# A new order for the first batch's attention, with fillers in the free columns of a PSUM bank

## The chip, the core and the metric

The kernel runs on one NeuronCore of a Trainium2 chip. The metric is the device time of one execution in microseconds (us). The span that a profile shows is some 1.8 us shorter than this time. All times compared here are of runs in the fast state; the one slow run (730.63 us, at a granted clock of 0.735) is left out, and one single run of unknown state is marked as such.

One derived number is used throughout. In the traces of all runs but the slow one the granted clock of TensorE stands at 1.00 or at 0.50 and nowhere between, and each run lists its mean. So the time that a run spent at half clock is (1 - granted clock) x span x 2. A clock of 0.994 over 578 us is 6.9 us. The clock is listed to three places, which makes this good to about 0.6 us. Values up to 1.2 us need not be a stretch inside the program: in one trace the only half clock begins at the very end.

## The reference, cut to what matters

```python
B, H, S, D = 8, 12, 448, 64                 # d_model = 12 * 64 = 768
q_n, k_n = rmsnorm(q, g_q), rmsnorm(k, g_k) # over D
attn = softmax(q_n @ k_n^T / sqrt(D))
x    = (attn @ v), heads side by side       # (8, 448, 768)
u    = x + (x^T @ U @ V)^T                  # U: 448x32, V: 32x448
out  = u + relu(u @ w_ch1) @ w_ch2          # 768 -> 3072 -> 768
```

Inputs and output are float32.

## The kernel before

Attention of batch b+1 is woven between the matmuls of batch b's MLP, so that TensorE nearly always has work. Only the first batch's attention has no MLP beside it. That stretch, the first 45 us, is `head()`: a plan written by hand, a list of pieces in one order. Each engine takes its own instructions in that order. A tile number t stands for four heads: q, k and v of heads 4t to 4t+3. A pair number p is two heads. The pieces that matter:

```python
def load_w1(i):                 # a piece of the first MLP weight, issued by POOL
    c = (slice(0, 512), slice(512, 1024), slice(1024, 2048), slice(2048, 3072))[i]
    nc.gpsimd.dma_start(w1b[:, :, c], w1r[:, :, c])

def cast_v(t):                  # v of four heads, f32 -> bf16; POOL
    nc.gpsimd.tensor_copy(va_of(t)[:, :, :, 0:D], vts.pop(t).rearrange(...))

def weigh(p, hh):               # attention weights times v; PE; needs va and E
    ...
    if hh and p < 6:
        o = ps_mm.tile([P, 4, D + 1], FP32, tag="mm")
    ...
    else:
        o = ps_o.tile([P, 4, D + 1], FP32, tag="o")
    ...

def heat(n):                    # fillers: matmuls of zeros that keep PE busy
    if n:
        warm = ps_mm.tile([P, 512], FP32, tag="mm")
        for _ in range(n):
            nc.tensor.matmul(warm, cold[:, 0:P], cold[:, 0:512], start=True, stop=True)

def head():
    load(0, 2); load(1); load(2)        # q and k of tiles 0, 1, 2; queue of SyncE
    load_mix()                          # U and V
    load_v(0); load_v(1); load_v(2)     # v; behind all of the above
    load(3); load_v(3)
    setup()                             # memsets on POOL
    plan = [(heat, 16), ..., (reduce, 1, ALL, (1,)), (load_w1, 0), ...,
            (cast_v, 0), ..., (weigh, 0, 1), ...]
    for fn, *args in plan:
        fn(*args)
```

Other pieces: `squares`, `reduce` and `rsqrt` make the norms, `scale` applies them (VectorE), `turn` transposes on PE and `keep` copies the result to SBUF, `scores` and `expo` are the softmax's matmuls and exponentials. From the fifteenth pair on the transposes are done by DMA instead (`qkT<-qkn`), and the mixer's input `u` as well (`u<-ring`).

Of the kernel before, what the change touches and what calls it, by code (L numbers as in the profile page):

```python
# [9 lines left out]
FP32 = mybir.dt.float32  # L10
# [7 lines left out]
def kernel(  # L18
# [13 lines left out]
    nc = tc.nc  # L32
    B, H, S, D = q.shape
# [5 lines left out]
    P = 128  # L39
# [26 lines left out]
    ps_mm = ctx.enter_context(tc.tile_pool(name="ps_mm", bufs=3, space=bass.MemoryType.PSUM))  # L66
    ps_s = ctx.enter_context(tc.tile_pool(name="ps_s", bufs=2, space=bass.MemoryType.PSUM))
    ps_o = ctx.enter_context(tc.tile_pool(name="ps_o", bufs=1, space=bass.MemoryType.PSUM))

    ident = consts.tile([P, P], BF16, name="ident")  # L70
    w1b = consts.tile([P, KD, dh], BF16, name="w1b")
# [46 lines left out]
    cold = ring[:, 0, :]  # L118
# [104 lines left out]
    ALL = slice(0, HG)  # L223
# [83 lines left out]
    def weigh(p, hh):  # L307

        b = p // 6
        par, g = b % 2, b // 2 % 2  # L310
        E, va = E_of(p), va_of(p // 2)
        hl = 2 * (p % 2) + hh
        if hh and p < 6:
            o = ps_mm.tile([P, 4, D + 1], FP32, tag="mm")
        elif hh and p % 6 == 5:
            o = ps_s.tile([P, 4, D + 1], FP32, tag="s", name="o")
        else:
            o = ps_o.tile([P, 4, D + 1], FP32, tag="o")
        for i, off in enumerate(OFFS[par]):
            n = (i + 1) % 4 if par == 0 and g else i  # L320
            for kc in range(NJ):
                c = PAD + kc * S + off
                nc.tensor.matmul(o[:, n, :], E[:, hh, c:c + P], va[:, hl, kc, :],  # L323
                                 start=(kc == 0), stop=(kc == NJ - 1))
        outs[p, hh] = o
# [333 lines left out]
    def head():  # L659

        A, Bh = slice(0, 2), slice(2, 4)
# [11 lines left out]
        cast_u = lambda: nc.gpsimd.tensor_copy(Uc, Uf)  # L673
        pool = nc.gpsimd
        plan = [
            (heat, 16),
            (grow2,),
            (squares, 0, A, (0,), pool),
            (squares, 0, A, (1,)),
            (squares, 0, Bh, (0,), pool),  # L680
            (reduce, 0, A, (0,)),
            (reduce, 0, A, (1,)),
            (reduce, 0, Bh, (0,)),
            (rsqrt, 0, A),
            (squares, 0, Bh, (1,)),
            (scale, 0, 0, (1,)),
            (reduce, 0, Bh, (1,)),
            (scale, 0, 0, (0,)),
            (rsqrt, 0, Bh),
            (scale, 0, 1, (1,)),  # L690
            (turn, 0),
            (squares, 1, ALL, (0,)),
            (gain,),
            (keep, 0, 0, 1),
            (yield_port, 0, 1),
            (squares, 1, ALL, (1,)),
            (keep, 0, 1),
            (scale, 0, 1, (0,)),
            (heat, 4),
            (scores, 0, (0,)),  # L700
            (turn, 1),
            (squares, 2, ALL, (0,)),
            (reduce, 1, ALL, (0,)),
            (expo, 0, 0),
            (scores, 0, (1,)),
            (reduce, 1, ALL, (1,)),
            (load_w1, 0),
            (expo, 0, 1),
            (rsqrt, 1),
            (heat, 2),  # L710
            (scores, 0, (2,)),
            (scores, 0, (3,)),
            (keep, 1, 1),
            (keep, 1, 0),
            (scale, 1, 0, (1,)),
            (squares, 2, ALL, (1,)),
            (scale, 1, 0, (0,)),
            (expo, 0, 2),
            (scale, 1, 1, (1,)),
            (heat, 5),  # L720
            (scores, 1, (0,)),
            (turn, 2),
            (scale, 1, 1, (0,)),
            (expo, 0, 3),
            (cast_u,),
            (expo, 1, 0),
            (scores, 1, (1,)),
            (scores, 1, (2,)),
            (load, 4),
            (heat, 2),  # L730
            (turn, 3),
            (expo, 1, 1),
            (scores, 1, (3,)),
            (keep, 2, 0),
            (expo, 1, 2),
            (keep, 2, 1),
            (expo, 1, 3),
            (scores, 2, (0,)),
            (yield_port, 1, 0),
            (scores, 2, (1,)),  # L740
            (cast_v, 0),
            (expo, 2, 0),
            (expo, 2, 1),
            (reduce, 2, ALL, (0,)),
            (reduce, 2, ALL, (1,)),
            (setup_u, 0),
            (scores, 2, (2,)),
            (scores, 2, (3,)),
            (keep, 3, 1),
            (rsqrt, 2),  # L750
            (setup_u, 1),
            (setup_u, 2),
            (cast_v, 1),
            (load_v, 4),
            (expo, 2, 2),
            (keep, 3, 0),
            (weigh, 0, 1),
            (scale, 2, 0, (0,)),
            (yield_port, 1, 1),
            (weigh, 0, 0),  # L760
            (expo, 2, 3),
            (scores, 3, (0,)),
            (scale, 2, 0, (1,)),
            (normalise, 0, 0),
            (scores, 3, (1,)),
            (normalise, 0, 1),
            (expo, 3, 0),
            (turn, 4),
            (weigh, 1, 0),
            (setup_u, 3),  # L770
            (expo, 3, 1),
            (keep, 4, 0),
            (normalise, 1, 0),
            (keep, 4, 1),
            (load, 5),
            (scores, 3, (2,)),
            (weigh, 1, 1),
            (scores, 3, (3,)),
            (expo, 3, 2),
            (expo, 3, 3),  # L780
            (weigh, 2, 0),
            (normalise, 1, 1),
            (scores, 4, (0,)),
            (gather, 0),
            (expo, 4, 0),
            (gather, 1),
            (scale, 2, 1, (0,)),
            (weigh, 2, 1),
            (gathered, 1, 1),
            (gathered, 0, 1),  # L790
            (scores, 4, (1,)),
            (load_v, 5),
            (scores, 4, (2,)),
            (setup_v,),
            (spread, 1),
            (scale, 2, 1, (1,)),
            (turn, 5),
            (load_w1, 1),
            (normalise, 2, 0),
            (normalise, 2, 1),  # L800
            (expo, 4, 1),
            (weigh, 3, 0),
            (yield_port, 2, 1),
            (spreaded, 1),
            (gather, 2),
            (scores, 4, (3,)),
            (expo, 4, 2),
            (keep, 5, 0),
            (expo, 4, 3),
            (cast_v, 2),  # L810
            (keep, 5, 1),
            (normalise, 3, 0),
            (gathered, 2),
            (scores, 5, (0,)),
            (weigh, 3, 1),
            (load_w1, 2),
            (spread, 0),
            (squares, 3, ALL, (1,)),
            (weigh, 4, 1),
            (scores, 5, (1,)),  # L820
            (normalise, 3, 1),
            (expo, 5, 0),
            (spreaded, 0, 1),
            (scores, 5, (2,)),
            (weigh, 4, 0),
            (normalise, 4, 1),
            (expo, 5, 1),
            (gather, 3),
            (spread, 2),
            (squares, 3, ALL, (0,)),  # L830
            (normalise, 4, 0),
            (gathered, 3, 1),
            (scores, 5, (3,)),
            (spread, 3),
            (spreaded, 2),
            (reduce, 3),
            (gather, 4),
            (expo, 5, 2),
            (squares, 4, ALL, (0,)),
            (cast_v, 3),  # L840
            (first, 0, (0, 1, 2), True),
            (expo, 5, 3),
            (weigh, 5, 1),
            (spreaded, 3, 1),
            (weigh, 5, 0),
            (first, 1, (0, 1, 2, 3), True),
            (rsqrt, 3),
            (normalise, 5, 1),
            (normalise, 5, 0),
            (gather, 5),  # L850
            (scale, 3, 0),
            (gathered, 4, 1),
            (gathered, 5, 1),
            (spread, 4),
            (first, 0, (3,), False),
            (spreaded, 4, 1),
            (spread, 5),
            (first, 0, (4,), False),
            (spreaded, 5, 1),
            (first, 1, (4,), False),  # L860
            (first, 0, (5,), False),
            (first, 1, (5,), False),
            (scale, 3, 1),
            (load_w1, 3),
        ]
        for fn, *args in plan:
            fn(*args)
# [33 lines left out]

    def heat(n):
        if n:
            warm = ps_mm.tile([P, 512], FP32, tag="mm")
            for _ in range(n):
                nc.tensor.matmul(warm, cold[:, 0:P], cold[:, 0:512], start=True, stop=True)

    def volume(b):
        n = (384, 512)[b % 2]
# [46 lines left out]
```

## Time and profile before

| | before |
|---|---|
| time, three runs | 579.06 us (578.95 to 579.19) |
| span of the profile, granted clock | 576.9 us, 0.993 |
| first MLP matmul issued by the MLP itself (`ph`) | 45.07 us |
| v of heads 0 to 3 landed, cast | 20.08, 20.31 us |
| first `weigh` | 24.68 us |

The prediction below shows the page and the stretches of the head. Lines of instructions show start, length, line, operation, tiles; in brackets how long the engine idled before, and for what. POOL's instructions in order of time (start, length, line, operation, tiles; in brackets how long the engine idled before, and for what):

```profile
16.12 1.02 POOL L181 DMA_DIRECT2D w1b<-in_moe_w_ch_dram  x1
...
20.31 1.03 POOL L221 CAST va<-vt 112x1024 bf16<-112x1024 f32 x1
```

The first weight piece is issued at 16.12. And PE up to its first `weigh`:

```profile
24.36 0.39 PE L172 MATMUL pt<-ident,Tw 32*128 32x32 bf16 x8
24.68 1.55 PE L323 MATMUL o<-va,E 112*128 112x65 bf16 x25
```

### The profile page before, as it was taken

The numbers are of one execution on the slowest core, as the hardware profiler recorded it, in microseconds if no ns is written. First come the engines' busy times: TensorE is split into PE (matmuls) and PEld (weight loads), VectorE is DVE, ScalarE is ACT, GpSimd is POOL, SyncE is SP. The second block draws the span as 40 slices with busy tenths as digits, with TensorE's granted clock in tenths as the row PEclk, the third lists the DMA queues.
The fourth block names the chain that finished last, engine by engine and source line by source line (L and its number), as shares of the span: only waits on it lengthen the run. The fifth ranks groups of instructions, "written<-read, shape, count | busy, mean of one in ns | idle before, by whom it ended". The sixth has DMA issues, their size and how long they took to land.

```text
span 576.9 us, 11306 instructions
## 1 busy us (share of the span) xinstructions
PE 560.0 (97%) x4607; PEld 306.5 (53%) x4607; DVE 387.1 (67%) x755; ACT 281.4 (49%) x419; POOL 79.0 (14%) x124
## 2 busy tenths in 40 slices
PE   5799999999999999999999999999999999999997
PEld 2465556544565555544465555644456555654464
DVE  4885964799875787647776598747767487453442
ACT  4777543376621875166641676246661475302200
POOL 4772510100020000000020000000011000000010
PEclk9799999999999999999999999999999999999999
DMA  9999985544443555544525455555334441050021
GB/s 212 243 252 226 216 139 141 129 118 88 112 136 93 117 135 126 114 99 113 129 75 116 105 130 120 125 132 128 82 79 127 122 97 33 28 110 1 1 55 55
DMA packets 103648, 67.22 MB, mean 117 GB/s; under 512 B 54716, under 2 KB 102060, under 8 KB 103596
## 3 DMA queue, kind: packets, MB, share of 16 engines
q1 hardware_dynamic: 93988, 56.77, 42.0%
q0 software_dynamic: 9376, 9.44, 9.8%
q8 instruction: 36, 0.59, 0.4%
q10 hardware_dynamic: 232, 0.30, 0.2%
q14 instruction: 16, 0.13, 0.1%
HBM read 52.19 MB, written 11.01 MB: 110 GB/s over the span
## 4 chain that ended last, share of the span: by engine, by line
PE 87%; DVE 4%; DMA 4%; ACT 1%; issue 0%; POOL 0%; DVEq 0%; ACTq 0%
PE ph L538 36%; PE pb L463 10%; PE po L463 8%; PE o L323 8%; PE pe L463 7%; PE pa L463 7%; PE sc L297 7%; DMA w1b<-in_moe_w_ch_dram 3%; DVE qkn L253 2%; PE pu L376 2%; ACT E L302 1%; DVE ring L378 1%; DMA u<-ring 1%; PE pm L362 1%; PE pt L264 0%
## 5 line engine op out<-in xcount | busy, mean ns | idle before, releaser
L538 PE MATMUL ph<-u,w1b 128*128 128x512 bf16 (+1 forms) x1128 | 232.6, 354 | 2.7 <-DVE qkT L275 1.2
L302 ACT ACTIVATE E<-sc 112x896 bf16<-112x896 f32 x184 | 159.8, 914 | 61.1 <-PE sc L297 61.0
L538 PEld LDWEIGHTS <-w1b 128*128 128x128 bf16 x1128 | 102.9, 98 | 110.9 <-issue 23.1
L463 PEld LDWEIGHTS <-hT 128*128 128x128 bf16 x1080 | 101.1, 98 | 71.1 <-issue 9.0
L541 ACT ACTIVATE hT<-ph 128x384 bf16<-128x384 f32 (+1 forms) x95 | 51.5, 542 | 130.7 <-PE ph L538 128.6
L543 DVE TENSOR_SCALAR hT<-ph 128x512 bf16<-128x512 f32 (+1 forms) x93 | 57.9, 622 | 57.0 <-PE ph L538 56.7
L323 PEld LDWEIGHTS <-E 112*128 112x128 bf16 x1472 | 59.8, 99 | 14.7 <-DVE ring L340 1.1
L323 PE MATMUL o<-va,E 112*128 112x65 bf16 x1440 | 62.1, 196 | 0.0
L253 DVE TENSOR_TENSOR qkn<-qk,rstd 112x512 bf16<-112x512 f32 x84 | 56.1, 707 | 7.2 <-ACT rstd L245 3.8
L297 PE MATMUL sc<-qkT 64*128 64x448 bf16 x384 | 55.9, 360 | 3.8 <-ACT E L302 2.2
L570 POOL COPY scratch<-qkn 1x1 bf16<-1x1 bf16 x44 | 11.1, 252 | 316.1 <-DVE qkn L253 316.1
L463 PE MATMUL po<-w2b,hT 128*128 128x384 bf16 x288 | 52.8, 326 | 0.1
L239 DVE TENSOR_REDUCE rstd<-sq 112x16 f32<-112x1024 f32 x40 | 48.4, 1211 | 4.7 <-ACT sq L231 4.7
L463 PE MATMUL pa<-w2b,hT 128*128 128x384 bf16 x264 | 49.5, 326 | 0.0
L463 PE MATMUL pb<-Tw,hT 128*128 128x384 bf16 x264 | 48.0, 326 | 0.0
L231 ACT ACTIVATE sq<-qk 112x1024 f32<-112x1024 f32 x36 | 38.2, 1061 | 8.1 <-DVE rstd L239 5.2
L378 DVE TENSOR_TENSOR ring<-pu,ring 128x768 bf16<-128x768 f32 (+3 forms) x36 | 31.0, 864 | 14.4 <-PE pu L376 13.8
L333 DVE RECIPROCAL rec<-o 128x4 f32<-128x4 f32 x96 | 17.1, 179 | 33.5 <-PE o L323 33.1
L340 DVE TENSOR_TENSOR ring<-o,rec 128x256 bf16<-128x256 f32 (+1 forms) x96 | 37.6, 391 | 2.4
L498 POOL TENSOR_TENSOR o<-o,ring 128x384 f32<-128x384 f32 x11 | 12.6, 1144 | 161.3 <-DVE o L497 161.3
L297 PEld LDWEIGHTS <-qkT 64*128 64x128 bf16 x384 | 12.7, 94 | 35.6 <-issue 32.0
L478 ACT ACTIVATE pb<-pa 128x384 f32<-128x384 f32 x11 | 5.2, 475 | 49.6 <-PE pa L463 49.6
(104 smaller groups left out, 424.1 us busy)
## 6 DMA issues: line engine op xcount, KB each, us to landing
qk<-in_k_dram SPq DMA_DIRECT2D x21, 448.0 KB, 5.4
vt<-in_v_dram SPq DMA_DIRECT2D x20, 448.0 KB, 4.7
qk<-in_q_dram SPq DMA_DIRECT2D x19, 448.0 KB, 3.8
w2b<-in_moe_w_ch_dram POOLq DMA_DIRECT2D x6, 768.0 KB, 14.8
w1b<-in_moe_w_ch_dram POOLq DMA_DIRECT2D x2, 1536.0 KB, 17.6
out_dram<-o SPq DMA_DIRECT2D x15, 168.0 KB, 2.3
out_dram<-o SPq DMA_DIRECT2D x16, 144.0 KB, 2.1
out_dram<-o SPq DMA_DIRECT2D x15, 120.0 KB, 2.1
```

What stands on the lines that cost most here:

```text
L231: nc.scalar.activation(sqs[t, s][:, hs], qks[t, s][:, hs], AF.Square)
L239: nc.vector.tensor_reduce(rstds[t][:, s, hs].rearrange("p h j -> p (h j)"), sqs[t, s][:, hs].rearrange("p h (j d) -> p (h j) d", d=D), AX, ...
L253: nc.vector.tensor_tensor(qkn[:, s].rearrange("p j h d -> p h j d"), qks[t, s][:, hp].rearrange("p h (j d) -> p h j d", d=D), rstd[:, s, h ...
L297: nc.tensor.matmul(sc[:, hh, 0:S], kT[pp, kc * SP:kc * SP + P], qT[pp, :], start=True, stop=True)
L302: nc.scalar.activation(E_of(p)[:, :, PAD + kc * S:PAD + (kc + 1) * S], scs.pop((p, kc))[0:SP, :, 0:S], AF.Exp, scale=float(D) ** 0.5)
L323: nc.tensor.matmul(o[:, n, :], E[:, hh, c:c + P], va[:, hl, kc, :], start=(kc == 0), stop=(kc == NJ - 1))
L340: nc.vector.tensor_tensor(ring[:, r0:r0 + t1 - t0, d0:d0 + D], o[:, t0:t1, 0:D], rec[:, t0:t1].rearrange("p c -> p c ()").to_broadcast([P, ...
L378: nc.vector.tensor_add(xv, pu[rows, 0:n, 0:HALF], xv)
L463: nc.tensor.matmul(ps, lhs[:, c, :], rhs[:, c, :], start=first and c == 0, stop=last and c == NC - 1, skip_group_check=again)
L538: nc.tensor.matmul(ph, w1b[:, dc, hc * P:(hc + 1) * P], u[:, dc, :], start=(dc == 0), stop=(dc == KD - 1))
L541: nc.scalar.activation(hT[:, hc, 0:n], ph, AF.Relu)
L543: nc.vector.tensor_relu(hT[:, hc, 0:n], ph)
```

## The change

Its intent is a head that takes less time and does not hang on exact timings: the order of the pieces was searched with random delays on every engine and load. Fillers move from a rotating PSUM tile to free columns of the bank that holds the attention output, so that they take no tile from transposes; they are shorter (240 columns) and many more (87 for 29). The first weight piece is issued right behind POOL's memsets. The diff, cut to its core:

```diff
+    bank = ps_o.tile([P, 512], FP32, name="bank")
+    even = bank[:, 0:4 * (D + 1)].rearrange("p (i d) -> p i d", i=4)
+    warm = bank[:, 272:512]
...
-            o = ps_o.tile([P, 4, D + 1], FP32, tag="o")
+            o = even
...
-            (heat, 16),
+            (heat, 34),
+            (load_w1, 0),
             (grow2,),
-            (squares, 0, A, (0,), pool),
...
-            (squares, 0, Bh, (0,), pool),
+            (squares, 0, A, (0,)),
+            (squares, 0, Bh, (0,)),
...
             (reduce, 1, ALL, (1,)),
-            (load_w1, 0),
... (some 200 lines: the same pieces in another order; heat of 1 to 6 in 14 places;
     load_w1 1 and 2 before yield_port 2, 1)
     def heat(n):
         if n:
-            warm = ps_mm.tile([P, 512], FP32, tag="mm")
             for _ in range(n):
-                nc.tensor.matmul(warm, cold[:, 0:P], cold[:, 0:512], start=True, stop=True)
+                nc.tensor.matmul(warm, cold[:, 0:P], cold[:, 0:240], start=True, stop=True)
```

## The prediction

> **What bounds the kernel now.** I read the page first, then one-microsecond stretches of the first 45 us, then each engine's instructions in time order there, then the DMA queues. The change touches only the head of the program (batch 0's attention and mixing up to its MLP), so the first question is what the head is worth. Span, busy shares, the PE and clock rows of the 40 slices, and the chain that ended last:
>
> ```profile
> span 576.9 us, 11306 instructions
> PE 560.0 (97%) x4607; PEld 306.5 (53%) x4607; DVE 387.1 (67%) x755; ACT 281.4 (49%) x419; POOL 79.0 (14%) x124
> ...
> PE   5799999999999999999999999999999999999997
> ...
> PEclk9799999999999999999999999999999999999999
> ...
> PE 87%; DVE 4%; DMA 4%; ACT 1%; issue 0%; POOL 0%; DVEq 0%; ACTq 0%
> ```
>
> From slice 3 on (a slice is 14.4 us) PE is at nine tenths and the chain is PE. Nothing after the head changes in program order, so the end moves by as much as the MLP of batch 0 starts earlier or later, less what a DMA takes back. Only slices 1 and 2 have room, and slice 2 has a granted clock of 0.7. By stretches (columns: length, then busy us with instruction count of PE, PEld, DVE, ACT, POOL, then clock, DMA share, GB/s):
>
> ```profile
> 10.00:12.00 2.00, 1.84 (x14) 1.01 (x14) 0.84 (x2) 1.44 (x2) 0.18 (x1) 1.00 1.10 248
> ...
> 19.00:23.00 4.00, 2.09 (x20) 1.04 (x19) 4.00 (x6) 2.75 (x5) 3.39 (x6) 1.00 1.14 250
> ...
> 24.00:30.00 6.00, 6.00 (x81) 4.32 (x80) 3.90 (x12) 3.84 (x7) 1.28 (x4) 0.51 1.17 256
> ```
>
> From 12 to 24 us VectorE is full and PE only partly (2.09 of 4 us in 19 to 23). Then the clock falls to a half and from 24 to 30 PE is full while VectorE (3.90) and ScalarE (3.84) wait for it. So the head is bound by VectorE first, then by a PE at half clock, then by VectorE and PE together, until the MLP's matmuls begin at 45.07. The chain adds one DMA:
>
> ```profile
> 33.48 16.77 DMA w1b<-in_moe_w_ch_dram
> 50.24 0.05 issue
> ```
>
> This is the third piece of the first MLP weight, issued at 33.48, landed at 50.24. PE idles only 0.27 us for it, so it and the head's compute end almost together: shortening one alone gives little. Further on, the fourth piece (issued 40.85, 18.4 us to landing, so about 59.2) is first needed at 65.67, and the second MLP weight at 80.20. Those have 6 us and more of slack.
>
> **What the Trainium skill says.** (1) "TensorE: Matmul & The Clock Gate", Part 1: the clock is half or full, set from the array's activity in windows of about 3.4 us. The trace agrees: 0.50 from 24 to 29, after 4 us at 52% PE busy. (2) "PSUM — Partial Sum Buffer", "PSUM bank collisions raise a hardware error": two engines on the same bank and quadrant collide even at different columns; rule 2 says a starting matmul clears the accumulate bits of its whole bank. The fillers share a bank with the attention output, but in the new order the last filler comes before the first weigh(p, 0), so neither can occur; the trace of before has no such sharing. (3) "DMA: Bandwidth & Descriptors", "Issuing engines are not separate DMA queues": all issuers' transfers interleave on the same 16 engines. The trace agrees: from 24 to 28 us the software queue moved 0.49 MB and the hardware queue 0.48, where from 8 to 12 the hardware queue alone had 0.99.
>
> **The change part by part.**
>
> Fillers. Before: 29 matmuls of 512 columns, 8.53 us of PE. After: 34+4+5+6+1+2+2+4+4+5+4+1+6+6+3 = 87 of 240 columns. That is 20,880 columns against 14,848. Four warm fillers took 1.04 us and five 1.25, so 512 columns cost 0.21 us; 6,032 more cost 2.5 us of PE. They are spread up to the third pair's scores, where before had none after 19.4 us, and PE idles there for 1.9 of 4 us. They should remove most of the half-clock stretch. They also no longer take one of three rotating PSUM tiles that transposes and gathers need. On the path: I put 0.3 us for fillers that delay a real matmul.
>
> The half-clock stretch. PE's work from 24 to 29.6 takes 5.6 us at half clock, so some 2.8 at full. VectorE then becomes the limit. Its idle time is what can be won: 2.1 us from 24 to 30, and about 1.7 from 30 to 42.2, when the last pair is normalised (summed from one-microsecond stretches). Of these 3.8 us I take 3.0: at some hand-overs VectorE still waits.
>
> load_w1(0). It moves from 16.12 us to just behind the memsets on POOL, which end at 4.55. Before, the software queue's first packets came some 6 us after the issue, so now at about 10.5 us. From then on the two queues have half each. The tile that waits is q of heads 4 to 7, which ScalarE needs ahead of the first exponential:
>
> ```profile
> 12.36 1.06 ACT L231 ACTIVATE w2b<-Tw 112x1024 f32<-112x1024 f32 x1 [0.32 <-DMA Tw<-in_q_dram]
> ```
>
> It landed at 12.36, so at 10.5 it has 1.9 us to go at full rate, and 3.8 at half: it lands at about 14.3. Loads behind it come up to 3.2 us later (0.79 MB of the weight at 0.125 MB/us is 6.3 us of sharing). In the new order this square still stands before the first exponential in ScalarE's queue, so exponentials begin 1.9 us later. VectorE has one 1.2 us reduction to fill this with, so 0.7 to 1.9 us are lost; I take 1.3.
>
> load_w1(1), load_w1(2). POOL stood from 24.45 to 32.37 waiting for a scaling (yield_port(2, 1), 7.0 us of it listed as idle), and the third piece came after that. The new order puts the piece ahead of that wait: POOL has squares of tile 2 (2 x 1.9), casts (0.74 + 2 x 1.03) and the issues (2 x 0.9) after about 17.5 us, so the third piece goes out at 27 to 28, six us earlier, and lands near 44. Worth 0.27 us by itself, and the condition for any larger gain.
>
> Moves between engines. Two half squares go from POOL (1.03 us each) to ScalarE (0.63 each), at a time when ScalarE idles 1.7 and 1.2 us for VectorE. One copy of keys (0.38) goes from VectorE to ScalarE and two gathered copies (0.28 each) net the other way. Sum: nothing, to 0.2 us.
>
> Sum for the start of the MLP: -3.0 + 1.3 + 0.3 - 0.3 = -1.7 us, and the same at the end, since the slacks named above are larger. 579.06 - 1.7 = 577.4; I lean a little toward the search having found more density than I can see, and say 577.2.
>
> **The rivals.** (a) The early weight load costs more than it gives: the late tile starves ScalarE and VectorE from 12 to 16 us, PE idles long enough to lose its clock right there, and since the work behind is VectorE-bound nothing is regained: 579 to 581. For it: VectorE was full from 12 to 24, and the DMA share is above 1 throughout. Against: the loads behind have slack, ScalarE idled over 5 us later on. (b) The order is dense: no half clock, VectorE and ScalarE back to back, and the MLP starts 4 to 5 us earlier: 574 to 575. For it: 24 exponentials of 0.86 us are only 20.6 us of ScalarE; VectorE's work up to the last normalisation is some 31 us. Against: VectorE is short by 1.3 us already at 14 us. (c) The gain comes and the DMA takes it: the head is faster, but the fourth weight piece and the second weight stay at the transfer rate (all queues together moved what they could until 84 us). With 6 us of slack this bites only at the far end of (b).
>
> **Range and chances.** (a) gives the upper end, (b) the lower: 573.8 to 580.2. Two per cent is 11.6 us, a quarter of the whole head, which neither reaches. Faster 0.01, same 0.98, slower 0.01.
>
> **What would show it.** Right: a granted clock near 1 from 20 to 30 us; the first weight issue at about 4.6 us and the square of tile 1's q waiting for its load until about 14; the third piece issued by 28 and landed before 45; the MLP's first matmul of the fifth column block at about 43 and all later stretches shifted by the same. Wrong: that tile on time at 12.4 (then the result is nearer 575); a new half-clock stretch at 14 to 20; a new DMA wait in the MLP at the fourth piece; or VectorE still idle for PE between 24 and 30.

## The result, and the profile after

The changed kernel took **580.8 us** (median of 580.09, 581.27, 580.32 and 581.96), the kernel before beside it 579.12 (578.95 to 580.29). The ratio is 1.0027, with a 95% interval from 1.0004 to 1.0049. A ratio here is the mean time of one kernel's fast runs over the mean of the other's in the same rounds, so it is not quite the ratio of the medians. Within 2%, as predicted, but 3.6 us above the predicted time and just outside its range.

The page of the kernel after, for the lines that the prediction shows of before:

```profile
span 578.3 us, 11392 instructions
PE 560.8 (97%) x4644; PEld 312.4 (54%) x4665; DVE 385.9 (67%) x756; ACT 282.7 (49%) x420; POOL 77.3 (13%) x122
...
PE   7899899999999999999999999999999999999997
...
PEclk9899999999999999999999999999999999999999
...
PE 91%; DVE 3%; ACT 2%; DMA 1%; issue 1%; POOL 1%; POOLq 0%; DVEq 0%; ACTq 0%
```

The weight piece has left the chain (DMA 4% to 1%), and slice 2's clock is 0.8 for 0.7. Yet the span is 1.4 us longer. The stretches of the head that answer to those of before:

```profile
19.00:23.00 4.00, 3.79 (x36) 2.12 (x35) 3.37 (x7) 3.97 (x8) 1.97 (x2) 1.00 1.12 236
23.00:25.00 2.00, 0.20 (x2) 0.03 (x1) 1.22 (x2) 1.88 (x3) 0.85 (x1) 1.00 1.12 245
25.00:29.00 4.00, 3.76 (x57) 2.99 (x57) 1.41 (x6) 0.93 (x2) 3.95 (x6) 0.57 1.12 252
```

From 19 to 23 us the fillers do what they are for: PE is busy for 3.79 of 4 us, where it was 2.09. Then from 23 to 25 PE has 0.20 us of work, and right after that the clock is a half (0.57 from 25 to 29), with VectorE and ScalarE starved. So the half-clock stretch has moved and become shorter (by the clock records of the traces 6.83 us from 23.07 before, 3.41 us from 25.20 now), with a hole ahead of it. What the hole waits for, first on PE and then on POOL:

```profile
22.72 0.48 PE L918 MATMUL bank<-ring 128*128 128x240 bf16 x3
25.24 0.98 PE L326 MATMUL bank<-va,E 112*128 112x65 bf16 x15 [2.05 <-POOL va L224]
```

```profile
4.50 0.99 POOL L184 DMA_DIRECT2D w1b<-in_moe_w_ch_dram  x1
...
24.15 1.04 POOL L224 CAST va<-vt 112x1024 bf16<-112x1024 f32 x1 [3.19 <-DMA vt<-in_v_dram]
```

PE waits 2.05 us for the cast of v, and the cast waited 3.19 us for the load of v. The trace's landing times say the same: v of heads 0 to 3 landed at 20.08 before and at 24.10 after. The load is issued at about 8 us in both. The tile that the prediction expected to be late was not, as ScalarE shows:

```profile
12.28 0.54 ACT L276 ACTIVATE qkT<-pt 128x448 bf16<-128x448 bf16 x1 [1.22 <-DVE qkT L274]
12.72 1.05 ACT L234 ACTIVATE w2b<-Tw 112x1024 f32<-112x1024 f32 x1
```

The square of that q has no wait for a DMA. Why it was on time and v was late is told by the queues. From 10 to 12 us before, then after (packets, MB, share of the 16 engines):

```profile
q1 hardware_dynamic: 503, 0.50, 110.4%
```

```profile
q1 hardware_dynamic: 370, 0.37, 79.8%
q0 software_dynamic: 114, 0.12, 34.2%
```

The software queue, which carries the weight, starts within this stretch and takes half from 12 us on (0.25 MB of 0.49 in the next two). All that it moves before v's turn is taken from the loads ahead of v.

Both kernels began the MLP at the same time, 45.07 and 45.16. So in these two profiles the head gained nothing, and what was lost was lost later. After 90 us PE has two waits that before has not, 1.44 and 0.76 us, and lacks one of 0.80. The MLP's second product began at 80.20 before and at 80.23 after, and 0.03 + 1.44 + 0.76 - 0.80 is the 1.4 us that is missing. The first of them comes from a transpose by DMA. Before (issue of the transpose, and the VectorE instruction that needs it), then after, with PE's wait:

```profile
225.92 1.22 SPq L284 DMA_TRANSPOSE qkT<-qkn  x1
...
228.90 0.34 DVE L289 TENSOR_SCALAR qkT<-qkT,gg 128x448 bf16<-128x448 bf16 x1 [1.85 <-DMA qkT<-qkn]
```

```profile
225.94 2.63 SPq L287 DMA_TRANSPOSE qkT<-qkn  x1
...
230.35 0.34 DVE L292 TENSOR_SCALAR qkT<-qkT,gg 128x448 bf16<-128x448 bf16 x1 [3.28 <-DMA qkT<-qkn]
...
231.47 0.67 PE L326 MATMUL bank<-va,E 112*128 112x65 bf16 x16 [1.44 <-DVE ring L343]
```

The same instruction at the same time took 2.63 us for 1.22. Before moves more data in the DMA view of 225.5 to 228.5 us (0.44 MB for 0.21, since the next load follows the shorter transpose), but one packet of another queue is there in the kernel after only:

```profile
q8 instruction: 1, 0.02, 3.5%
```

That packet is 16 KB of instructions. There are 36 of this queue in both traces, one about every 14 us on average, and TensorE's program before is 2 x 4607 = 9,214 instructions, about 36 x 256. The Trainium skill has the reason in "Runtime: NRT & Kernel Launch", section "Instruction fetch mechanics": an engine's instructions are refilled by DMA in blocks of 16 KiB, or 256 instructions, at a cost that it calls mostly hidden. The program after is 116 instructions longer, since short fillers need more instructions, so each later fetch comes at another moment of the program. In the trace after, nine transposes are lengthened by over 0.25 us, each beside such a packet; before, one. Five more overlap a packet in the trace after and are not lengthened, so the packet is not enough by itself.

So there are two theories.

- **V (late values).** The early weight load takes bandwidth from v; `weigh` waits; PE's clock falls; the head gives back what the fillers won.
- **F (fetches).** The longer TensorE program moves the instruction fetches onto the DMA transposes, and these waits are the loss.

The expectations below call V "theory L". Their rival J is that long transposes are chance, and rival C that the shared bank or the new order costs the time itself.

### The profile page after: what moved, and what is told of

It is laid out like the page before. It is cut to its first block, busy times and chain, and to the rows that moved or that the text cites. A ratio compares the mean times of both kernels' runs of the same rounds, so it can differ in the third digit from the quotient of the medians.

```text
span 578.3 us, 11392 instructions
## 1 busy us (share of the span) xinstructions
PE 560.8 (97%) x4644; PEld 312.4 (54%) x4665; DVE 385.9 (67%) x756; ACT 282.7 (49%) x420; POOL 77.3 (13%) x122
## 4 chain that ended last, share of the span: by engine, by line
PE 91%; DVE 3%; ACT 2%; DMA 1%; issue 1%; POOL 1%; POOLq 0%; DVEq 0%; ACTq 0%
PE ph L541 36%; PE pb L466 11%; PE po L466 8%; PE pe L466 7%; PE bank L326 7%; PE pa L466 7%; PE sc L300 7%; PE pu L379 2%; DVE qkn L256 1%; PE o L326 1%; ACT E L305 1%; PE bank L918 1%; DMA qkT<-qkn 1%; PE first L892 1%; PE pm L365 1%
## 5 line engine op out<-in xcount | busy, mean ns | idle before, releaser
L541 PE MATMUL ph<-u,w1b 128*128 128x384 bf16 (+1 forms) x1107 | 230.9, 353 | 3.8 <-DVE qkT L278 1.5
L326 PE MATMUL bank<-va,E 112*128 112x65 bf16 x1280 | 54.5, 195 | 3.5 <-POOL va L224 2.0
L343 DVE TENSOR_TENSOR ring<-bank,rec 128x192 bf16<-128x192 f32 (+1 forms) x83 | 32.3, 389 | 1.9
L336 DVE RECIPROCAL rec<-bank 128x4 f32<-128x4 f32 x83 | 14.7, 178 | 26.0 <-PE bank L326 25.5
```

The lines of the kernel that those rows point to most:

```text
L326: nc.tensor.matmul(o[:, n, :], E[:, hh, c:c + P], va[:, hl, kc, :], start=(kc == 0), stop=(kc == NJ - 1))
L343: nc.vector.tensor_tensor(ring[:, r0:r0 + t1 - t0, d0:d0 + D], o[:, t0:t1, 0:D], rec[:, t0:t1].rearrange("p c -> p c ()").to_broadcast([P, ...
L541: nc.tensor.matmul(ph, w1b[:, dc, hc * P:(hc + 1) * P], u[:, dc, :], start=(dc == 0), stop=(dc == KD - 1))
```

## The experiments

All ran with the kernel before on the same chip. In each round of experiments the kernel before ran 11 times; its medians were 579.79, 580.05, 579.95 and 580.61 us.

| kernel | median us (range) | ratio to before (95%) | mean us at half clock |
|---|---|---|---|
| after, fillers of 512 (`a_wide`) | 579.62 (577.83 to 581.62) | 0.9993 (0.9966 to 1.002) | 5.1 |
| before, 104 more instructions (`b_narrow`) | 580.52 (578.61 to 581.96) | 1.001 (0.9986 to 1.0033) | 8.5 |
| after, weight late (`a_w1_late`) | 578.88 (578.07 to 580.75) | 0.9988 (0.9966 to 1.001) | 0.6 |
| after, v first (`a_v0_first`) | 580.03 (578.92 to 582.09) | 1.001 (0.9985 to 1.0035) | 4.1 |
| both (`a_w1_late_wide`) | 579.29 (578.02 to 579.81) | 0.9986 (0.9974 to 0.9998) | 5.8 |
| before, weight early (`b_w1_early`) | 583.06 (581.73 to 583.89) | 1.0054 (1.0041 to 1.0067) | 10.7 |
| before, more fillers in the bank (`b_fill`) | 580.15 (577.8 to 580.8) | 0.9999 (0.9973 to 1.0025) | 4.0 |
| after, weight between (`a_w1_mid`) | 580.13 (578.31 to 583.06) | 1.0007 (0.9977 to 1.0037) | 2.7 |
| `a_w1_mid`, 50 more instructions (`a_w1_mid_p25`) | 577.75 (575.46 to 578.93) | 0.9957 (0.9928 to 0.9986) | 0.2 |
| the same again | 577.63 (576.73 to 578.99) | 0.9956 (0.994 to 0.9973) | 1.7 |
| after, 50 more instructions (`after_p25`) | 581.62 (578.12 to 582.7) | 1.0006 (0.9979 to 1.0034) | 6.6 |
| after, unchanged, second time | 580.13 (577.15 to 582.4) | 1.0001 (0.9977 to 1.0025) | 5.0 |
| third time | 578.5 (577.57 to 581.14) | 0.9981 (0.9955 to 1.0008) | 1.2 |
| fourth time | 580.74 (578.01 to 583.36) | 1.0006 (0.9978 to 1.0034) | 6.2 |

### First round: take each theory's cause away

**a_wide** gives the program before's length back (9,228 instructions, for 9,214): 36 fillers of 512 columns over the whole bank instead of 87 of 240.

```diff
-    warm = bank[:, 272:512]
+    warm = bank[:, 0:512]
-            (heat, 34),
+            (heat, 16),
... (14 more, each about halved)
-                nc.tensor.matmul(warm, cold[:, 0:P], cold[:, 0:240], start=True, stop=True)
+                nc.tensor.matmul(warm, cold[:, 0:P], cold[:, 0:512], start=True, stop=True)
```

> The changed kernel with 36 fillers of 512 columns (the whole bank, which nothing else uses until the first weigh) in place of 87 of 240, at the same places: 51 pairs of weight load and matmul fewer, so that the TensorE program is as long as in the kernel before (within 2 instructions). Theory F (fetch phase: TensorE's instructions come in by DMA in blocks of 16 KB, and the 103 more instructions of the change moved those fetches onto the DMA transposes, which then take 1.2 to 1.4 us longer): the MLP of batch 0 still starts at 45.2 +- 0.6, but at most 3 transposes overlap a fetch, the waits of 1.44 us (attention output of batch 3) and 0.76 us (MLP of batch 3) are gone, time 579.2 +- 0.6. Rival J (the long transposes are chance of each execution) and rival C (the shared bank or the new order costs the time itself): time stays at 580.8 +- 0.6.

Its profiled run was the slow one, so its profile is not used; the five fast runs give a ratio of 0.9993. **b_narrow** does the opposite to the kernel before: its order untouched, 104 instructions more on TensorE, for as many columns.

```diff
-            (heat, 16),
+            (heat, 68, 120),
```

> The kernel before with its first 16 fillers of 512 columns split into 68 of 120 columns (same columns in all, in a place where TensorE has nothing else to do): 104 instructions more in the TensorE program, nothing else changed. Theory F: the head is the same (MLP of batch 0 starts at 45.1 +- 0.3), but 6 or more transposes overlap an instruction fetch and are long, as in the changed kernel, and the time is 580.5 +- 0.7. Rivals J and C: 579.1 +- 0.5, and the long transposes stay at 1 or 2.

The mechanism of F is there: the kernel before now has lengthened transposes where the kernel after has them (at 123.7, 245.7, 266.2 us, up to 2.62 us long), and waits of PE at 233.29 (0.99 us) and 249.58 (0.48). The time is another matter: 1.001, with an interval that holds both no loss and all of it. And the head did not stay the same, though that was expected: in the profiled run PE waited 2.63 us for a scaling on VectorE that took 2.98 us, and the MLP started at 47.71. So this time tests F only loosely. **a_w1_late** puts the weight load back to where the kernel before has it.

```diff
             (heat, 34),
-            (load_w1, 0),
...
             (reduce, 1, ALL, (1,)),
+            (load_w1, 0),
```

> The changed kernel with the first piece of the first MLP weight loaded where the kernel before does it (after the reductions of tile 1), nothing else. Theory L (the early weight load makes the values of heads 0 to 3 land 3 us late, the cast and the first weigh wait for them, and TensorE loses its clock in that wait): the cast of these values no longer waits over 0.5 us, first weigh at 23.3 or earlier instead of 25.24, no half clock between 22 and 30, MLP of batch 0 starts 1 to 2 us earlier (43.2 to 44.2), and time is 1 to 2 us below the changed kernel (579.3 +- 0.7). Rival (the order itself is not denser; something else, VectorE or the scores, ends the head): MLP start 45.0 or later, time 580.8.

POOL, then PE, then VectorE of this profile:

```profile
21.21 1.03 POOL L224 CAST va<-vt 112x1024 bf16<-112x1024 f32 x1
```

```profile
24.41 0.48 PE L918 MATMUL bank<-ring 128*128 128x240 bf16 x3
24.73 0.67 PE L326 MATMUL bank<-va,E 112*128 112x65 bf16 x16
```

```profile
18.24 2.98 DVE L256 TENSOR_TENSOR qkn<-Tw,rstd 112x512 bf16<-112x512 f32 x1
```

The wait is gone as V has it: neither the cast nor `weigh` waits, and none of the six runs has more than 1.2 us of half clock. But the first `weigh` came at 24.73, not by 23.3 as expected, and the gain in time is too small to be told from none (0.9988): a new cost takes the place of the wait. The scaling on VectorE at 18.24 took 2.98 us; the same one in the kernel after took 0.68 (at 17.96). POOL's squares of tile 2, held back by the weight's issue ahead of them on POOL, now run beside it, from 18.75 to 20.66. The Trainium skill names this in "SBUF — State Buffer", section "Who interferes with whom": a VectorE instruction with two SBUF inputs contends with a POOL instruction that reads SBUF. The trace agrees, at 2.3 us. The kernel before had the same collision at 17.25 (2.38 us). The MLP starts at 43.97, and a 0.93 us wait at 229.81, from F, is still there. **a_v0_first** takes the lateness of v away in another way: its load goes ahead of those for tile 2 and the mixer, the weight stays early.

```diff
         load(1)
+        load_v(0)
         load(2)
         load_mix()
-        load_v(0)
```

> The changed kernel with the early weight load kept, but the values of heads 0 to 3 loaded ahead of tile 2 and of U and V. Theory L: the values land about 5 us earlier, the cast waits for nothing but its own order, first weigh by 23.5, MLP of batch 0 starts at 43.2 to 44.5, time 579.3 +- 0.8. If tile 2, now 1.8 us later, becomes the new wait (its squares are ahead of the cast in the queue of POOL), the gain is under 0.5 us and the squares of tile 2 show the wait.

The wait moved to the tile that now stands behind: POOL's squares of tile 2 waited 13.42 us for their k and began at 18.91, VectorE and PE waited in turn, the MLP started at 46.28 and the clock fell as before. What matters is thus not v alone. The weight's 0.79 MB come ahead of something that the head needs, whichever it is.

### Second round: both, and the same move in the kernel before

**a_w1_late_wide** has both edits, of `a_w1_late` and of `a_wide`.

> Both edits at once: the first weight piece late, and 36 wide fillers so that the TensorE program is as long as before. If the late weight piece is what keeps the clock (theory L) and the length is what decides the overlaps of transposes and instruction fetches (theory F), both hold together: half clock at most 3.5 us in every run, at most 3 overlaps that lengthen a transpose, MLP of batch 0 at 43.5 to 44.3, fast runs 577.5 +- 0.7, ratio to before 0.996. If only L holds: 578.9 as a_w1_late. If the wide fillers delay real matmuls: MLP start 44.5 or later.

One lengthened transpose remains, and the time is that of `a_w1_late` (0.9986 and 0.9988): taking F away as well adds nothing that can be seen. But the expectation on the clock failed: half clock is 3.5 to 6.9 us in all five runs. In the profile no cast of v is behind it. PE waited 1.55 us for the scaling on VectorE, which took 2.98 us beside POOL again, and the half clock begins at 21.65, 0.4 us after that wait. So a late weight does not keep the clock by itself. **after_again** is the kernel after, unchanged.

> The changed kernel itself on the chip of these runs, to compare with. Both theories: 580.5 +- 0.7, half clock between 3 and 11 us in its runs, 8 or more long transposes at the same places as in its first profile (225.9, 238 to 244, 264, 294, 384, 446, 479 us). Rival J (the long transposes are chance): other places, another number.

It now measures the same as before (1.0001), with the same lengthened transposes in the profile. The first 1.0027 was one draw of four. **b_w1_early** makes the disputed move alone, in the kernel before. TensorE's program is not touched at all, so F has no part in it.

```diff
             (heat, 16),
+            (load_w1, 0),
             (grow2,),
...
             (reduce, 1, ALL, (1,)),
-            (load_w1, 0),
```

> The kernel before with the first weight piece loaded right after the memsets, as in the changed kernel, nothing else; TensorE's program is the same, instruction for instruction. Theory L: loads behind it come 3 us later, so the order of before waits for the values of heads 0 to 3 as well: the cast at 23.5 to 24.5 instead of 20.31, first weigh 26 to 28 instead of 24.68, MLP of batch 0 at 46 to 48, half clock 7 us or more in most runs, time 580.5 to 582. Rival (the early load is harmless where the order is denser): 579.5 +- 0.5, MLP start 45.

The effect on the time is the clearest: 1.0054, and the whole interval above 1; 3.1 us of 580. The path is not the expected one. POOL and VectorE early on, then PE up to its first `weigh`, then the casts on POOL:

```profile
5.51 2.04 POOL L233 TENSOR_TENSOR w2b<-qk 112x512 f32<-112x512 f32 x2
```

```profile
6.22 1.50 DVE L672 TENSOR_TENSOR grow<-grow 1x128 f32<-1x128 f32 x1 [6.22 <-DMA grow<-in_g_k_dram]
```

```profile
11.53 0.93 PE L264 MATMUL pt<-ident,qkn 112*128 112x112 bf16 x8 [2.59 <-DVE qkn L253]
...
26.65 1.56 PE L323 MATMUL o<-va,E 112*128 112x65 bf16 x25
```

```profile
23.46 1.04 POOL L221 CAST va<-vt 112x1024 bf16<-112x1024 f32 x1 [0.90 <-DMA vt<-in_v_dram]
25.45 1.04 POOL L221 CAST va<-Tw 112x1024 bf16<-112x1024 f32 x1 [0.95 <-DMA Tw<-in_v_dram]
```

Both casts wait for their loads, and v lands 3.3 us later than before (23.41 for 20.08). But `weigh` has no wait: v was cast at 24.50, over 2 us ahead of it. The MLP starts at 46.92, 1.85 us late, and 1.5 us of this is there at the first transpose (11.53 for 10.03), when the weight had moved almost nothing (first packet at 10.31). The weight's issue on POOL (4.50 to 5.49) stands ahead of the two half squares, which now run beside the first work of VectorE: it took 1.50 us for 0.28, after a small load that itself landed 0.7 us later. PE waited 2.59 us and was at half clock from 10.99 to 17.82, and again from 24.64. The rest of the loss comes after the head: the third weight piece, issued at 35.32 for 33.48, made PE wait 1.30 us for 0.27. Together, 1.85 + 1.03 us, this is nearly all of the 3.0 us between the two spans. So the run shows that the early issue is dear in the order of before. It does not show V, and the kernel after, whose ScalarE has these half squares, has not this path.

**a_wide_again** was one look for the profile that `a_wide` had lost.

> a_wide once more for a profile in the fast state, since its first one fell in a slow state. Theory F: at most 3 transposes lengthened by a fetch, none at 225.9 and 238 to 244; no wait of TensorE over 0.5 us for the attention output or for u in batch 3. Rivals J and C: as many as in the changed kernel, 8 or more.

With the program as long as before's, the lengthened transposes at 226, 239, 264, 294, 384 and 446 us are gone, and so are their waits. But v came at 24.64, `weigh` waited 3.15 us, the MLP started at 47.81, and the run took 581.68. That is one run, of unknown state, so its time says little; the profile says that F's cure leaves V's loss.

### Third round: the fillers alone, and a better place for the weight

**b_fill** tests the prediction's largest gain by itself: the order of before, the fillers moved to the bank, and eight more where PE idles from 19 to 23 us.

```diff
+    bank = ps_o.tile([P, 512], FP32, name="bank")
+    even = bank[:, 0:4 * (D + 1)].rearrange("p (i d) -> p i d", i=4)
-            o = ps_o.tile([P, 4, D + 1], FP32, tag="o")
+            o = even
-            (heat, 2),
+            (heat, 6),
             (turn, 3),
...
             (scores, 1, (3,)),
+            (heat, 3),
...
             (scores, 2, (2,)),
+            (heat, 1),
             (scores, 2, (3,)),
-                nc.tensor.matmul(warm, cold[:, 0:P], cold[:, 0:512], start=True, stop=True)
+                nc.tensor.matmul(bank, cold[:, 0:P], cold[:, 0:512], start=True, stop=True)
```

> The kernel before in its own order, with its fillers written to the bank of the attention output (free until the first weigh) and 8 more of 512 columns where TensorE idled from 19.4 to 23 us: nothing of the new order, nothing of the early weight. It measures the step 'the half-clock stretch' by itself. As the prediction sized it (VectorE idles 3.8 us for a half-clock TensorE, 3.0 of it won): no half clock from 23 to 30, MLP of batch 0 at 42 to 42.8, time 576.5 to 577.5. Rival (the stretch costs little, because other hand-overs follow it closely): MLP start 43.8 to 45, time 578 to 579.5.

It gained nothing: 0.9999, outside both forecasts of MLP start and time. Half clock fell to 4.0 us a run, but in the profiled run it came earlier, because PE had stood still ahead of the new fillers (for a scaling on VectorE that took 3.18 us). PE's line, and the stretches from 17 us:

```profile
19.33 0.93 PE L266 MATMUL pt<-ident,qkn 112*128 112x112 bf16 x8 [2.75 <-DVE qkn L255]
```

```profile
17.00:19.00 2.00, 0.00 (x0) 0.00 (x0) 2.00 (x2) 0.78 (x1) 2.00 (x3) 0.94 1.13 230
19.00:23.00 4.00, 3.67 (x17) 1.56 (x18) 4.00 (x7) 1.73 (x2) 1.36 (x2) 0.50 1.15 233
```

A filler that stands in the order behind a matmul that waits cannot fill that wait. Fillers at half clock then delay the real work: `pt` and `sc` come late, and the MLP starts at 47.22. **a_w1_mid** puts the weight load of the kernel after behind POOL's squares of tile 2, so that it neither starts early nor, as was hoped, pushes these squares onto the scaling.

```diff
             (heat, 34),
-            (load_w1, 0),
...
             (squares, 2, ALL, (1,)),
+            (load_w1, 0),
             (load, 4),
```

> The changed kernel with the first weight piece behind the last squares of tile 2 on POOL. In a_w1_late the piece stood ahead of these squares, and a scaling on VectorE that ran beside them took 2.98 us instead of 0.68. If that was a hold-up by POOL's work, here this scaling takes under 1.1 us, the cast of the first values follows at 21.5 to 22.5 without waiting for its load, first weigh at 22.8 to 23.5, MLP of batch 0 at 42.8 to 43.6 (a_w1_late: 43.97), half clock at most 3.5 us, time 578 +- 0.7. If not: MLP start 44 or later.

Its profile has the earliest MLP start of all (43.31), but the rounds give 1.0007, with runs from 578.31 to 583.06. Most of the expectation failed: the scaling still took 2.38 us, v landed only at 22.82 and its cast waited 1.59 us for it, and one run had 8.1 us of half clock. And the head, once early, met the next limit, the third weight piece (issued at 25.97, landed at 50.28):

```profile
50.32 1.15 PE L541 MATMUL ph<-u,w1b 128*128 128x384 bf16 x6 [2.06 <-DMA w1b<-in_moe_w_ch_dram]
```

**a_w1_mid_p25** adds 50 instructions on TensorE to that, to move the fetches on: 59 fillers of 138 columns instead of 34 of 240 at the very start.

```diff
-            (heat, 34),
+            (heat, 59, 138),
```

> a_w1_mid with its first 34 fillers of 240 columns as 59 of 138 columns (the same columns, where TensorE has nothing else to do): 50 instructions more, so every later instruction fetch falls about 3 us earlier in the work. From the trace of a_w1_late I estimate the overlap of fetches and transposes at 10 us for its length and 4 us for this one. Theory F: the same head as a_w1_mid within 0.5 us, 3 to 5 lengthened transposes instead of 8 or more, none at the qkT transpose of 225 us; time 0.3 to 1.2 us below a_w1_mid. Rival: same number of lengthened transposes, same time.

It was faster than before, 0.9957 with the interval below 1. Its profile has two lengthened transposes, for seven, and PE's wait for the third weight piece is 0.28 us, for 2.06. Five of six runs show no half clock at all. **after_third** is the kernel after once more.

> The changed kernel once more on the chip of these three. 580.3 +- 0.7, half clock 3 to 10 us in most runs; MLP of batch 0 in its profile at 45 to 46.2; the cast of the first values waits 2 us or more for its load.

This time the kernel after did well (0.9981), against the expectation, and its profile goes with it. PE's first `weigh`, then its stretch:

```profile
24.51 0.67 PE L326 MATMUL bank<-va,E 112*128 112x65 bf16 x16 [1.62 <-POOL va L224]
```

```profile
25.00:29.00 4.00, 4.00 (x83) 2.91 (x80) 3.77 (x13) 3.38 (x5) 3.94 (x6) 1.00 1.13 261
```

v had landed at 23.37; PE waited 1.62 us and kept its clock (1.00, for 0.57 in the first profile).

### Fourth round: is it the fetches or the clock?

What was open: had the 50 instructions helped through the fetches, or had those rounds been lucky with the clock? **after_p25** adds them to the kernel after, where the weight load is early.

> The changed kernel with only its first 34 fillers of 240 columns cut into 59 of 138 (the same columns): 50 TensorE instructions more, nothing else. Theory F for the changed kernel itself: 3 to 5 lengthened transposes instead of 8 or more, the wait in batch 3 (0.77 to 1.44 us in three profiles) gone, and at the same half-clock time 1 to 1.6 us less than the changed kernel of these rounds. The late values stay: cast at 23.4 to 25, half clock in some runs. Rival (the overlap costs nothing in the end, the difference of a_w1_mid and a_w1_mid_p25 was luck): the same time within 0.5 us at the same half-clock time.

Three transposes are lengthened, and the wait near 230 us vanished, yet the time was 1.0006. v landed at 25.59, `weigh` waited 3.36 us, the MLP started at 48.69. **after_fourth** is the kernel after beside it.

> The changed kernel, to compare after_p25 with. From its 16 fast runs so far: 578.1 in runs without half clock, and 0.4 us more for each us of it; 8 or more lengthened transposes.

1.0006 again, with five lengthened transposes (expected were 8 or more) and a wait of 1.15 us near 233. So in this order moving the fetches gained nothing that the rounds can show. The overlap of F and its waits are there, but as the main cause of the time it falls. **a_w1_mid_p25_again** repeats the fast version on a second draw.

> The version that was ahead of both, on another draw of chip: half clock under 1.5 us in at least 5 of 6 runs, 577.5 +- 0.8, ratio to before 0.995 to 0.998. If the first result was luck of the chip: half clock of 3 us or more in most runs, and 579 or more.

0.9956, as the first time: 2.6 us less than before. The expectation on the clock failed (half clock under 1.5 us in three of six runs, not in five), so the clock alone is not the reason. Its POOL has the weight issued behind the squares of tile 2, and v 3 us earlier than the kernel after:

```profile
18.19 1.02 POOL L184 DMA_DIRECT2D w1b<-in_moe_w_ch_dram  x1
...
21.14 1.04 POOL L224 CAST va<-vt 112x1024 bf16<-112x1024 f32 x1 [1.71 <-DMA vt<-in_v_dram]
```

This run and `after_p25` of the same round differ in one line, the place of the weight load, and are the cleanest test of the early load in the new order. Their means are 577.68 and 580.88: 3.2 us (95% interval 1.3 to 5.1, from their six runs each), with v landing at 21.09 for 25.59, no wait ahead of `weigh` for 3.36 us, the MLP starting at 44.12 for 48.69, and 1.7 us of half clock a run for 6.6. The same pair without the 50 instructions, `a_w1_mid` and the kernel after in the third round, gives 1.5 us the other way, inside its noise (plus or minus 1.9): in the profiles of that round the kernel after had v early, at 23.37, and `a_w1_mid` waited for the third weight piece.

### What the runs say together

The profiles with the early weight load in the order after and the fillers of 240 or fewer columns, the unchanged kernel four times and `after_p25`:

| v landed, us | PE's wait ahead of first `weigh` | MLP starts | half clock in that run |
|---|---|---|---|
| 23.37 (third) | 1.62 | 43.41 | 0 |
| 24.10 (first) | 2.05 | 45.16 | 3.5 |
| 25.02 (second) | 2.54 | 46.08 | 3.5 |
| 25.09 (fourth) | 3.04 | 47.26 | 7.0 |
| 25.59 (`after_p25`) | 3.36 | 48.69 | 10.4 |

The order is the same in every column. (`a_wide_again`, with other fillers, does not fit it: v at 24.64, a wait of 3.15 us, the MLP at 47.81, 10.4 us of half clock. So the landing is not all that sets the wait.) 2.2 us between the first and the last landing become 5.3 us at the start of the MLP, because the wait is followed by half clock in four of the five. Behind the MLP's start all sixteen profiles but the slow one need nearly the same: 531.5 to 533.2 us (before 531.8, after 531.8 to 533.1), while its start varies from 43.3 to 48.7. Two of the three that need 533 us or more are the two in which PE waits over 1 us for the third weight piece. So most of the variation arises in the head.

Over all rounds, 44 runs of the kernel before have a mean of 580.08 us and 9.2 us at half clock; 22 runs of the kernel after have 580.01 and 4.6. By time at half clock, the kernel after takes:

| half clock, us | runs | mean time after | runs | mean time before |
|---|---|---|---|---|
| none (up to 1.2) | 8 | 578.16 | 0 | |
| 2 to 6 | 4 | 579.77 | 5 | 578.76 |
| 6 to 9 | 6 | 581.01 | 16 | 579.98 |
| 9 to 13 | 4 | 582.46 | 18 | 580.23 |
| over 13 | 0 | | 5 | 581.14 |

The change halves the time at half clock, but at an equal amount of it the kernel after is 1.0 to 2.2 us slower. The two cancel. (These groups are sorted by what happened in a run, so they do not show what half clock costs: in the kernel after it comes along with a wait for v.)

## Why the prediction was wrong

- **The early weight load: this step failed.** The prediction put it at +1.3 us, on the grounds that "The tile that waits is q of heads 4 to 7" and that "the loads behind have slack". That q was on time: the software queue's packets had only just begun. (The prediction had this among its signs and expected a time "nearer 575" from it; the opposite came.) The loads behind it had no slack. v of heads 0 to 3 landed 3.3 to 5.5 us later than before in the five profiles of the table, and PE stood 1.62 to 3.36 us for it. In the new order the step was worth 3.2 us where it was moved alone and clear of noise (`after_p25` against `a_w1_mid_p25_again`), and could not be told from nothing in the third round. That v comes late and PE waits is thus shown; what it costs in time is not fixed by the two pairs together. Moved alone in the kernel before it cost 3.1 us (ratio 1.0054), but there by the order on POOL and the third weight piece, not by v. The prediction's own figures, "up to 3.2 us later" and a cast at 20.31 us without a wait, were enough to ask which later tile would be needed next, and by whom. Its rival (a) named the size and the loss of the clock; it was dismissed for that supposed slack, and the place was 23 to 25 us instead of 12 to 16.
- **The half-clock stretch (-3.0 us): too large, and not independent of the step above.** The fillers hold the clock up to 23 us, as predicted. Then the wait for v makes the stretch again. In the eight runs without it the kernel after has a mean of 578.16, which is 1.9 us under before's mean. That is near the predicted sum of -1.7, though not a proof of its terms: the eight are picked by their outcome, and five of them are from one round. The other fourteen runs average 581.07 (22 x 580.01 less 8 x 578.16, over 14). The prediction added a cost and a gain that are not independent: where v was late enough, the clock was lost (four of five profiles). And fillers alone, in the order of before, gained nothing (`b_fill`, 0.9999).
- **Fillers (+0.3 us on the path).** Not measured apart: with the late weight, fewer and wider ones left the ratio as it was (0.9986 and 0.9988, in different rounds), but half clock came back (5.8 us a run for 0.6). Their count had an effect that the prediction did not think of, the phase of the instruction fetches. In the first profiles this is 1.4 us of waits. Over the profiles it is less: the MLP's start to the end averages about 0.4 us more in kernels with many lengthened transposes (532.4 for 532.0), which is within their spread.
- **The third weight piece (-0.3 us).** Half right: issued at 27.14, within the 27 to 28 predicted, and gone from the chain. But it landed at 48.31, not near 44, and so only 1.9 us earlier than before. In before it was needed 4.95 us after the MLP's start, so by this estimate a head two us shorter would have met it again, as `a_w1_mid` did (2.06 us). This is rival (c), with another piece of the weight than it named.
- **Moves between engines (0 to 0.2 us).** Not tested alone. The pairing of POOL's squares with a scaling on VectorE turned out to be worth up to 2.5 us of VectorE when it goes wrong (3.18 us for 0.68 in `b_fill`). It stood in the trace of before, at 17.25 (2.38 us).
- **The range.** It came from the rivals alone, and stopped at 580.2, short of the 581 that rival (a) allowed. Runs of one kernel, the same code, go from 577.15 to 583.36 for the kernel after, a spread as wide as the whole range of 6.4 us. The mean over all its rounds, 580.01, is inside the range by 0.2 us and 2.8 above the predicted time; the first median, 580.8, is outside.

**What stays open.** How much the overlaps of fetches and transposes cost on average; the experiments bound it only to a fraction of 1%. Why `a_w1_mid_p25` beats `a_w1_mid` by more than the half clock accounts for: in the third round it had 2.5 us less, which at 0.40 us per us (the slope of a line through the 22 runs of the kernel after) is 1.0 of the 2.9 us between their means. The wait for the third weight piece, 2.06 us in one profile and 0.28 in the other, would cover most of the rest, if it is as long in the runs without a profile. And what makes v land 2 us earlier or later from one run to the next. The load counts as landed with the last of its 16 parts. In the semaphore records of the five profiles the last part comes 1.7 to 2.0 us after the one before it in three (24.10 after 22.36 in the first), and 0.9 and 0.4 us in the others; in before 0.2 us. In all five a fetch of instructions (0.9 to 1.4 us) runs during v's load, at 17.0 to 20.6 us; in before it comes at 27.04, after it. So F may reach into the head through v. No run separates this, and `b_w1_early`, with no fetch there, still had v at 23.41.

## What to carry to other kernels

When a transfer is moved earlier, follow every transfer that stands behind it to the instruction that needs it, and ask what the most critical engine does meanwhile: here waits of 2.05 to 3.36 us brought back the half clock that the rest of the change had removed. A move by itself in another order is not the same step: `b_w1_early` lost as much as expected, by another path, and only its profile says so. Fillers hold a clock only through waits that stand behind them in the engine's order, and their number moves every later instruction fetch. And where runs of one kernel spread by 1%, a difference of 0.3% needs several separate draws before it is explained.

## What the Trainium skill lacked or had wrong

- "TensorE: Matmul & The Clock Gate", Part 1, says of the slow start of a kernel that its penalty is under 1% of a typical span and that no exact count should be fitted. For half clock later on the size here is alike: the kernel after's runs with 9 to 13 us of it took 4.3 us more than those with none, 0.7% of the span. But it decided the result here. The half-clock stretches in the heads of the profiles are 3.41, 6.83, 10.24 and 13.65 us long, which agrees with its window of about 3.4 us. What it lacks is a figure for waits shorter than this window: waits of 1.62 us (`after_third`) and 1.87 us (before, at 10.03) kept the clock, and waits of 1.55 us (`a_w1_late_wide`) and 2.05 us (after) went with its loss.
- "Runtime: NRT & Kernel Launch", "Instruction fetch mechanics", calls a fetch mostly hidden. No page says that a fetch beside a DMA transpose goes with a longer transpose: 2.63 us for 1.22, and 5.42 for 4.18 for a group of three; nine of the fourteen that overlap a fetch in the trace after.
- "DMA: Bandwidth & Descriptors", "Latency and other measured facts", has about 1 us to the first byte of a transfer issued by POOL. Here the weight piece issued at 4.50 showed its first packets at about 10.7 us, and the one issued at 16.12 at about 22.2, with the hardware queue full in both cases: some 6 us. In `a_w1_mid_p25` it was 3.4 us (18.38 to 21.76).
- "SBUF — State Buffer", "Who interferes with whom", was right and has no figure for this pair: a 0.68 us scaling on VectorE took 2.38 to 3.18 us beside POOL's squares.
